# First pair's tiles in the order of work, sign rows in one VectorE instruction, the mixture's scale chain first in line

## The chip, the cores and the metric

The kernel runs on one core of a Trainium2 chip. A core has TensorE (PE, matmuls and transposes into PSUM), VectorE (DVE), ScalarE (ACT), GpSimd (POOL) and SyncE (SP, which here issues every DMA). Each engine works through its own list in order and waits on semaphores for the others. The metric is the device time of one execution in microseconds, the median of several runs. All times below are of the device.

## The reference, cut to what matters

Two layers. The first is attention for 4 batches of 8 heads over 768 positions of width 64, in which a query sees only the keys that fall into the same bucket. The bucket is the pattern of signs of six random projections:

```python
q_bits = (np.einsum('bhsd,dk->bhsk', q, proj) > 0)
k_bits = (np.einsum('bhsd,dk->bhsk', k, proj) > 0)
mask = q_bucket[:, :, :, None] == k_bucket[:, :, None, :]
scores = np.where(mask, scale * np.matmul(q, k.transpose(0, 1, 3, 2)), -1000000000.0)
attn_out = softmax(scores) @ v
```

The second is a mixture of four causal attention experts over the first layer's output `x` (4 x 768 x 512), of which each position takes the two with the largest gate:

```python
logits = x @ w_gate                      # the two largest of four, softmax over them
for e in range(E):
    q, k, v = x @ wq[e], x @ wk[e], x @ wv[e]
    ye = softmax(causal(scale * q @ k.T)) @ v @ wo[e]
    out += gate[e] * ye
```

## The kernel before, in words

The work is cut into units. `("L", b, h)` is one head of the first layer, `("M", b, e)` one expert of the second; there are 32 of the one and 16 of the other, in one sequence in which the experts of a batch stand between the heads of the next. A unit computes scores twice. `max_steps` makes them in `mx` tiles (PSUM, two buffers) and VectorE reduces each to a maximum per query (`pm`, or `pmw` for the first four heads). `shift_steps` turns the maxima into a `row` that a DMA writes under the query tile as one more contraction row. `s_unit` then makes the scores again, transposed, in `st` tiles (three buffers); ScalarE takes the exponential twice, once to fp32 (`p`) and once to fp16 (`ph`), GpSimd subtracts one from the other (`pl`, function `lo`), and TensorE multiplies `ph` and `pl` with the halves of V into `o`. `normalise` divides (`rden`, then `xp` or `yn`).

The bucket mask is part of the matmul. The six projections of q and k are made by TensorE with the small matrix `pbd`, four groups of 32 PSUM rows in one tile; `signs` turns them into 0/1 style rows and DMAs (`qk<-M`, `qk<-Mw`, `xt<-Mw`) write those under q and k, so that a score in another bucket falls out. Before the change VectorE compared and subtracted (`m0` in the code, `m` in the profile) and ScalarE scaled the result into `M`. In the very first pair of heads the four groups were worked as four instructions of 32 rows on each engine.

Heads are prepared in pairs: `prep_wide` for the first two pairs of batch 0 (fp32 tiles, named `xt` for pair 0 and `qk` for pair 1), `prep_pair` for the rest. They transpose q and k (`natq`, `natk`), split each into two parts, project and make the sign rows. `natq`, `natk`, `natv` are loaded by SP; a load waits for a mark that `FIRST` names (for instance "m", the last sign instruction). `pair_scales` finds scales from the maxima of q, k and v (`mqk`). `mixture_scales(b)` makes three numbers per batch (`xs`) that the experts need: a reciprocal and a product on VectorE in a `misc` tile of PSUM, a copy on ScalarE (`xw`), a product on VectorE (`xs<-misc,xw`), two more on ScalarE. Every transpose, projection and scale shares the two `misc` buffers.

Everything is first recorded and then put in order by `Recorder.schedule`, a list scheduler with its own costs: at each step the instruction that can start first on its engine goes, and among equals the one with the smaller number `prio`, which is the place of recording plus an entry of `PRIO` for the group that it belongs to. So every change in costs or priorities redraws the order of all engines. Until the first `o` tile the scheduler fills idle TensorE time with small matmuls `o<-ident`, as many as its own estimate of the gap asks for; they compute nothing that is used. All instructions are issued by one line of the code (L423), so the profile's rows are told apart by tiles.

Of the kernel before, what the change touches and what calls it, by code (L numbers as in the profile page):

```python
# [141 lines left out]
PRIO = {"norm": -300, "pair_scales": -100, "shift_steps": -100, "halves": 50, "weights": 400}  # L142
# [286 lines left out]
WIDE = 2.0 ** 60  # L429
LN_SHIFT = 5.545177444479562  # L430
# [7 lines left out]
FIRST = {("q", 1): None, ("k", 1): "m", ("v", 1): "row", ("q", 2): "m", ("k", 2): "m"}  # L438
# [13 lines left out]
def tile_kernel(ctx, tc, q, k, v, proj, w_gate, wq, wk, wv, wo, out):  # L452
# [75 lines left out]

    pat = con.tile([1, 3, 128], BF, name="pat")
# [3 lines left out]
    nc.gpsimd.memset(pat[:, 1], MISS)  # L533
    nc.gpsimd.memset(pat[:, 2], 1.0)
    for g in range(4):
        o = 32 * g
        if g < 2:
            nc.gpsimd.memset(pat[:, 0, o + 2 * NB:o + 2 * MR], 1.0)
        else:
            nc.gpsimd.memset(pat[:, 0, o:o + 2 * NB], 1.0)  # L540
            nc.gpsimd.memset(pat[:, 0, o + 2 * MR:o + 2 * MR + 4], -1.0)
            nc.gpsimd.memset(pat[:, 1, o + 2 * MR:o + 2 * MR + 4], UNIT)
            nc.gpsimd.memset(pat[:, 2, o:o + 2 * MR], WIDE)
# [3 lines left out]
    sub_mul = con.tile([128, 3], FT, name="sub_mul")  # L547
    nc.vector.tensor_copy(sub_mul, pp[:, 0:3])
# [6 lines left out]
    pbh = con.tile([128, 32], HF, name="pbh")  # L555
    pbl = con.tile([128, 32], HF, name="pbl")
# [155 lines left out]
    def signs(p, gs, ds, parts, M, mul, rows):  # L712

        m0 = sb.tile([128, HS], HF, name="m0", bufs=1)
        for r in parts:
            nc.vector.tensor_scalar(m0[r], p[r, :HS], 0.0, sub_mul[r, 0:1], op0=OP.is_gt, op1=OP.subtract)
            marks["m"] = nc.scalar.activation(M[r], m0[r], AF.Copy, scale=sub_mul[r, mul:mul + 1])
        for g in gs:
            a, n = (ds[g % 2]["qa"], MR) if g < 2 else (ds[g % 2]["ka"], MR + rows)
            move(a[D:D + n].rearrange("p (j s) -> p j s", j=2), M[32 * g:32 * g + 2 * n][:, None, :])  # L720

    def prep_wide(hp):
# [14 lines left out]
        for nm, h in [("q", 0), ("q", 1), ("k", 0), ("k", 1)] if hp else [("q", 0), ("k", 0), ("q", 1), ("k", 1)]:  # L737
# [17 lines left out]
            gs = () if nm == "q" else range(4) if hp and h else () if hp else (h, 2 + h)  # L755
            if gs:
                p = misc()
                for g in gs:
                    marks["p"] = nc.tensor.matmul(p[32 * g:32 * g + 32, :HS], pbd, TT["q" if g < 2 else "k"][:, g % 2],
                                                  start=True, stop=True, tile_position=(0, 32 * g))  # L760
                signs(p, gs, ds, [slice(0, 128)] if hp else [slice(32 * g, 32 * g + 32) for g in gs], M, 2, 1)
# [5 lines left out]
    def proj_halves():  # L767
# [9 lines left out]
        t = sb.tile([128, 32], FT, name="pbs", bufs=1)  # L777
# [6 lines left out]
    def prep_pair(b, hp):  # L784
# [32 lines left out]
        for n, (w, x) in enumerate(((pbh, 0), (pbl, 0), (pbh, 1))):  # L817
            for g in range(4):
                nc.tensor.matmul(p[32 * g:32 * g + 32, :HS], w, parts[g][x], start=not n, stop=n == 2,
                                 tile_position=(0, 32 * g))  # L820
        signs(p, range(4), ds, [slice(0, 128)], sb.tile([128, HS], HF, name="M", bufs=1), 1, 2)
# [158 lines left out]
    def s_unit(u):  # L980
# [477 lines left out]
```

## Time and profile before

| what | us |
|---|---|
| median of 3 runs | 663.68 (663.67 to 669.59) |
| the profiled execution | 664.07 |
| its span, first to last instruction | 662.3 |
| TensorE busy | 634.6 (96%) |
| VectorE busy | 513.4 (78%) |
| ScalarE busy | 509.1 (77%) |
| GpSimd busy | 467.2 (71%) |

Some 1.8 us of the profiled execution lie outside its span. Busy TensorE time includes the filling matmuls of the start.

### The profile page before, as it was taken

How to read it: one execution, taken by the hardware profiler on the slowest of the kernel's cores; microseconds unless marked ns; L12 is line 12 of the kernel's file. 1: busy time of each engine (PE TensorE's matmuls, PEld its weight loads, DVE VectorE, ACT ScalarE, POOL GpSimd, SP SyncE). 2: the span in 40 equal slices, each digit the busy share in tenths (PEclk: the TensorE clock that was granted, in tenths of full speed). 3: DMA queues.
4: the chain of work that ended last, by engine and by line, in shares of the span. 5: the costliest groups of instructions: out<-in, count | busy, mean ns of one | idle time of the engine just before them, and what ended most of it. 6: DMA issues, size and time to landing. Idle time of an engine off the chain costs nothing. (4 is left out here: it accounts for less than half of the span.)

```text
span 662.3 us, 21568 instructions
## 1 busy us (share of the span) xinstructions
PE 634.6 (96%) x8320; PEld 466.9 (70%) x8320; DVE 513.4 (78%) x1280; ACT 509.1 (77%) x1093; POOL 467.2 (71%) x496
## 2 busy tenths in 40 slices
PE   8999999899999999999999999999999899999996
PEld 7878777576777666677767777777767666767663
DVE  5978999899779797878978898877967569447641
ACT  3278899899968978786977889795978777942773
POOL 3088999798966967784966869784866776960662
PEclk9999999799999999999999999999999999999999
DMA  4674454434330323333052332305154012001212
GB/s 101 137 160 93 100 120 100 98 68 117 67 86 11 82 66 72 77 64 90 21 139 90 65 87 63 91 9 113 39 125 116 9 42 57 3 22 35 75 66 96
DMA packets 109923, 50.87 MB, mean 77 GB/s; under 512 B 88428, under 2 KB 105980, under 8 KB 109820
## 3 DMA queue, kind: packets, MB, share of 16 engines
q1 hardware_dynamic: 109820, 49.50, 31.9%
q8 instruction: 65, 1.06, 0.7%
q14 instruction: 38, 0.31, 0.2%
HBM read 20.98 MB, written 6.29 MB: 41 GB/s over the span
## 5 line engine op out<-in xcount | busy, mean ns | idle before, releaser
L423 POOL TENSOR_TENSOR pl<-p,ph 128x512 f16<-128x512 f32 (+2 forms) x384 | 424.1, 1128 | 168.4 <-ACT ph L423 90.2
L423 ACT ACTIVATE p<-st 128x512 f32<-128x512 f32 (+2 forms) x384 | 229.8, 599 | 45.0 <-PE st L423 38.1
L423 DVE TENSOR_REDUCE pm<-mx 128x2 f32<-128x512 f32 (+2 forms) x380 | 227.1, 616 | 23.8 <-PE mx L423 21.6
L423 PE MATMUL st<-qk 78*128 78x512 f16 (+2 forms) x976 | 227.3, 325 | 3.5 <-DMA qk<-row 2.1
L423 ACT ACTIVATE ph<-st 128x512 f16<-128x512 f32 (+2 forms) x384 | 230.3, 602 | 0.2 <-PE st L423 0.2
L423 PEld LDWEIGHTS <-ph 128*128 128x128 f16 x2976 | 157.8, 98 | 30.8 <-issue 3.4
L423 PEld LDWEIGHTS <-qk 78*128 78x128 f16 (+4 forms) x1392 | 124.5, 98 | 60.9 <-issue 12.4
L423 PE MATMUL mx<-qk 76*128 76x512 f16 (+2 forms) x488 | 136.6, 326 | 7.7 <-DVE pm L423 3.1
L423 PEld LDWEIGHTS <-pl 128*128 128x128 f16 x1488 | 136.2, 97 | 10.2 <-POOL pl L423 4.0
L423 PE MATMUL o<-vh,pl 128*128 128x65 f16 x1152 | 127.0, 194 | 2.0 <-POOL pl L423 1.4
L423 PE MATMUL o<-vh,ph 128*128 128x65 f16 x1152 | 127.7, 194 | 0.1
L423 PE MATMUL o<-vl,ph 128*128 128x64 f16 x1152 | 126.8, 192 | 0.1
L423 PE MATMUL misc<-xt,wqk_h 128*128 128x384 f16 x256 | 53.7, 326 | 0.0
L423 PEld LDWEIGHTS <-ident 128*128 128x128 bf16 x499 | 38.4, 101 | 12.0 <-issue 2.2
L423 PE MATMUL o<-mvh,ph 128*128 128x65 f16 x336 | 37.2, 194 | 0.9 <-DVE yn L423 0.6
L423 PE MATMUL o<-mvh,pl 128*128 128x65 f16 x336 | 37.5, 193 | 0.0
L423 PE MATMUL o<-mvl,ph 128*128 128x64 f16 x336 | 37.2, 192 | 0.0
L423 ACT ACTIVATE qk<-misc 128x384 f16<-128x384 f32 (+1 forms) x31 | 15.2, 489 | 28.4 <-PE misc L423 26.3
L423 PEld LDWEIGHTS <-xt 128*128 128x128 f16 x324 | 30.2, 97 | 8.6 <-ACT xt L423 0.5
L423 DVE SCALAR_TENSOR_TENSOR qk<-misc,qk 128x384 f16<-128x384 f32 (+1 forms) x34 | 18.8, 553 | 21.3 <-ACT qk L423 21.1
L423 PEld LDWEIGHTS <-wqk_h 128*128 128x128 f16 x256 | 24.3, 97 | 14.7 <-issue 0.6
L423 DVE SCALAR_TENSOR_TENSOR qk<-misc,cs,qk 128x384 f16<-128x384 f32 x56 | 32.9, 603 | 0.9 <-ACT qk L423 0.7
(181 smaller groups left out, 948.1 us busy)
## 6 DMA issues: line engine op xcount, KB each, us to landing
qk<-qk SPq DMA_DIRECT2D x128, 96.0 KB
natv<-in_v_dram SPq DMA_DIRECT2D x16, 384.0 KB
natq<-in_q_dram SPq DMA_DIRECT2D x15, 384.0 KB
natk<-in_k_dram SPq DMA_DIRECT2D x15, 384.0 KB
qk<-qk SPq DMA_DIRECT2D x112, 48.0 KB
out_dram<-ot SPq DMA_DIRECT2D x20, 256.0 KB
xt<-xt SPq DMA_DIRECT2D x8, 96.0 KB
xt<-xt SPq DMA_DIRECT2D x4, 192.0 KB
```

Of the source, the lines that this page charges most:

```text
L423: getattr(getattr(self.nc, e), m)(*[real(x) for x in args], **{k: real(x) for k, x in kw.items()})
```

## The change

Six edits. (1) `mixture_scales` gets a priority of -3000, ahead of all else that is ready. (2) `signs` becomes one VectorE instruction that compares with a small number and multiplies by a number per partition, and writes `M` itself; the ScalarE step goes. `pat`, from which the per-partition numbers are made, is filled by more small memsets, and `pbd` has a second half with negated signs. (3) The groups stand as q and k of one head, then q and k of the other, so the first pair needs one instruction of 64 rows for each head, and the DMAs go in the order q, k of the first head, q, k of the second. (4) The tiles of the first pair are taken from their ring in the order head by head. (5) The load of pair 1's k waits for mark "t" (a split) and no longer for "m". (6) In the last unit the subtraction that makes `pl` may go to VectorE or GpSimd.

```diff
-PRIO = {"norm": -300, "pair_scales": -100, "shift_steps": -100, "halves": 50, "weights": 400}
+PRIO = {"norm": -300, "pair_scales": -100, "shift_steps": -100, "halves": 50, "mixture_scales": -3000, "weights": 400}
...
+LEAST = 2.0 ** -126
...
-FIRST = {("q", 1): None, ("k", 1): "m", ("v", 1): "row", ("q", 2): "m", ("k", 2): "m"}
+FIRST = {("q", 1): None, ("k", 1): "t", ("v", 1): "row", ("q", 2): "m", ("k", 2): "m"}
...
-    pbd = con.tile([128, 32], FT, name="pbd")
+    pbd = con.tile([128, 2, 32], FT, name="pbd")
     nc.gpsimd.memset(pbd, 0.0)
     for j in range(2):
-        for r in range(2):
-            nc.vector.tensor_copy(pbd[D * j:D * j + D, 2 * NB * r + j:2 * NB * r + 2 * NB:2], pst[D * j:D * j + D])
+        for i in range(2):
+            for r in range(2):
+                x = pbd[D * j:D * j + D, i, 2 * NB * r + j:2 * NB * r + 2 * NB:2]
+                if i == r:
+                    nc.vector.tensor_copy(x, pst[D * j:D * j + D])
+                else:
+                    nc.vector.tensor_scalar(x, pst[D * j:D * j + D], -1.0, None, op0=OP.mult)
...
-    def signs(p, gs, ds, parts, M, mul, rows):
+    def signs(p, gs, ds, part, M, mul, rows):
-        m0 = sb.tile([128, HS], HF, name="m0", bufs=1)
-        for r in parts:
-            nc.vector.tensor_scalar(m0[r], p[r, :HS], 0.0, sub_mul[r, 0:1], op0=OP.is_gt, op1=OP.subtract)
-            marks["m"] = nc.scalar.activation(M[r], m0[r], AF.Copy, scale=sub_mul[r, mul:mul + 1])
+        marks["m"] = nc.vector.tensor_scalar(M[part], p[part, :HS], least_times[part, 0:1], least_times[part, mul:mul + 1],
+                                             op0=OP.is_gt, op1=OP.mult)
         for g in gs:
-            a, n = (ds[g % 2]["qa"], MR) if g < 2 else (ds[g % 2]["ka"], MR + rows)
+            a, n = (ds[g // 2]["ka"], MR + rows) if g % 2 else (ds[g // 2]["qa"], MR)
...
-        for n in "qk":
-            for d in ds:
+        for n, d in [(n, d) for n in "qk" for d in ds] if hp else [(n, d) for d in ds for n in "qk"]:
...
-                signs(p, gs, ds, [slice(0, 128)] if hp else [slice(32 * g, 32 * g + 32) for g in gs], M, 2, 1)
+                signs(p, gs, ds, slice(32 * gs[0], 32 * gs[-1] + 32), M, 2, 1)
...
-                nc.gpsimd.tensor_tensor(pl[:, :o], p32[:, :o], ph[:, :o], op=OP.subtract)
+                (nc.vector_or_gpsimd if u == seq[-1] else nc.gpsimd).tensor_tensor(pl[:, :o], p32[:, :o], ph[:, :o], op=OP.subtract)
```

How the order moves is shown at three places. Over the whole program TensorE loses 40 of its 307 filling matmuls and keeps all its other matmuls; ScalarE loses 19 sign activations; GpSimd gets 14 more memsets and gives five of the last unit's six `pl` to VectorE.

The first place is VectorE's list at the start, before the change, from the second head's signs (`m`) through the first head's nine reductions (`pmw_151`) to its row (`roww`):

```order
L423 TENSOR_SCALAR m_347<-misc,sub_mul 32x384 x2
L423 TENSOR_SCALAR qk<-misc 128x384
L423 SCALAR_TENSOR_TENSOR qk<-misc,qk 128x384
L423 TENSOR_SCALAR qk<-misc 128x384
L423 SCALAR_TENSOR_TENSOR qk<-misc,qk 128x384
L423 TENSOR_REDUCE pmw_151<-mx 128x2 x9
L423 TENSOR_REDUCE pmw_153<-mx 128x2
L423 TENSOR_REDUCE negm_138<-pmw_151 128x12
L423 TENSOR_REDUCE pmw_153<-mx 128x2 x2
L423 TENSOR_SCALAR roww<-misc 6x128
```

The same stretch of the changed kernel (its numbers for the tiles differ; `pmw_178` are the first head's maxima, `pmw_180` the second's):

```order
L423 TENSOR_SCALAR Mw<-misc,least_times 64x384
L423 TENSOR_SCALAR qk<-misc 128x384 x2
L423 SCALAR_TENSOR_TENSOR qk<-misc,qk 128x384 x2
L423 TENSOR_REDUCE pmw_178<-mx 128x2 x9
L423 TENSOR_REDUCE pmw_180<-mx 128x2
L423 TENSOR_REDUCE negm_157<-pmw_178 128x12
L423 COPY Tk<-misc 128x384
L423 TENSOR_REDUCE pmw_180<-mx 128x2
L423 TENSOR_TENSOR qk<-misc,qk 128x384 x2
L423 TENSOR_REDUCE pmw_180<-mx 128x2
L423 TENSOR_SCALAR roww<-misc 6x128
```

Two instructions of signs became one, and a copy and two splits of pair 1's k moved between the first head's maxima and its row.

The second place is SP's list of DMAs around the loads of pair 2, before the change, where `natq`, `natk` and `natv` in the second half are pair 2's and `qk<-Mw` are pair 1's sign rows:

```order
L423 DMA natv<-in_v_dram 128x12x64
L423 DMA xt<-xt 64x384 x2
L423 DMA qk<-Mw 12x2x384 x2
L423 DMA qk<-Mw 13x2x384 x2
L423 DMA natq<-in_q_dram 128x12x64
L423 DMA xt<-roww 1x6x128
L423 DMA fq_113<-fr 2x6x128
L423 DMA xt<-xt 64x768
L423 DMA natk<-in_k_dram 128x12x64
```

And in the changed kernel:

```order
L423 DMA natv<-in_v_dram 128x12x64
L423 DMA qk<-Mw 12x2x384
L423 DMA qk<-Mw 13x2x384
L423 DMA qk<-Mw 12x2x384
L423 DMA qk<-Mw 13x2x384
L423 DMA xt<-xt 64x384 x2
L423 DMA natq<-in_q_dram 128x12x64
L423 DMA natk<-in_k_dram 128x12x64
```

The sign rows alternate q and k, and the load of pair 2's k stands right behind that of q, ahead of three DMAs that it followed.

The third place is VectorE's list in batch 1, before the change, from the second instruction of `mixture_scales` (`misc<-misc,rw`) to the one that frees its `misc` tile (`xs<-misc,xw`):

```order
L423 TENSOR_SCALAR misc<-misc,rw 128x1
L423 SCALAR_TENSOR_TENSOR xt<-misc,xs,xt 128x3x128
L423 TENSOR_SCALAR up<-misc,lower 12x128
L423 SCALAR_TENSOR_TENSOR row<-misc,up 12x128
L423 TENSOR_REDUCE mqk<-natq 128x1
L423 TENSOR_SCALAR rden<-o,cs_2259 128x6
L423 RECIPROCAL rden<-rden 128x6
L423 TENSOR_TENSOR xp<-o,rden 128x6x64
L423 TENSOR_REDUCE mqk<-natk 128x1
L423 TENSOR_REDUCE pm_147<-mx 128x2 x2
L423 TENSOR_TENSOR xs<-misc,xw 128x1
```

And in the changed kernel, from the chain's first instruction:

```order
L423 RECIPROCAL misc<-xs 128x1
L423 TENSOR_TENSOR rden<-o,gw 128x6
L423 SCALAR_TENSOR_TENSOR qk<-misc,cs_2277,qk 128x384
L423 TENSOR_SCALAR misc<-misc,rw 128x1
L423 TENSOR_TENSOR yn<-o,rden 128x6x64
L423 TENSOR_TENSOR xs<-misc,xw 128x1
```

Ten instructions stood between the two before, one does now. In batch 3 it is 19 before and two after.

## Rows read from the trace of the kernel before

**Rows 1.** The page, part 1: busy time by engine, share of the span, instructions.

```profile
PE 634.6 (96%) x8320; PEld 466.9 (70%) x8320; DVE 513.4 (78%) x1280; ACT 509.1 (77%) x1093; POOL 467.2 (71%) x496
```

**Rows 2.** Engines by stretch: length, busy us (instructions), then clock, DMA share, GB/s.

```profile
40.00:60.00 20.00, 18.74 (x229) 15.54 (x228) 16.39 (x37) 15.18 (x32) 15.95 (x16) 0.91 0.56 118
80.00:100.00 20.00, 19.78 (x286) 14.53 (x285) 19.94 (x39) 19.04 (x40) 18.21 (x17) 1.00 0.54 117
120.00:140.00 20.00, 18.17 (x196) 12.43 (x194) 17.27 (x39) 17.35 (x38) 17.04 (x16) 0.83 0.30 66
140.00:160.00 20.00, 18.39 (x231) 12.52 (x230) 17.05 (x37) 18.35 (x47) 16.72 (x18) 1.00 0.56 126
```

**Rows 3.** Whom TensorE waited for: us in total, times, longest us.

```profile
PE st L423 <- DMA qk<-row: 2.1, 2, 1.2
...
PE o L423 <- POOL pl L423: 1.4, 3, 0.6
```

**Rows 4.** Timeline of the start: start us, length us, what [idle before <-releaser].

```profile
7.65 0.49 PE L423 MATMUL misc<-ident,natk 128*128 128x128 f32 x3
12.15 1.23 ACT L423 ACTIVATE Mw<-m,sub_mul 32x384 fp32r<-32x384 f16 x2
12.77 1.99 SPq L423 DMA_DIRECT2D xt<-Mw  x2
16.72 0.71 PE L423 MATMUL mx<-xt 76*128 76x512 f32 x3
18.37 6.30 DVE L423 TENSOR_REDUCE pmw<-mx 128x2 f32<-128x512 f32 x9
26.68 0.27 DVE L423 TENSOR_SCALAR roww<-misc 6x128 fp32r<-6x128 f32 x1
34.19 0.15 DVE L423 TENSOR_SCALAR cs<-misc 128x1 int32<-128x1 int32 x1
```

**Rows 5.** Timeline around pair 2's k: its load, its maximum, TensorE's next `mx`.

```profile
38.78 0.53 SPq L423 DMA_DIRECT2D natk<-in_k_dram  x1
44.22 0.95 DVE L423 TENSOR_REDUCE mqk<-natk 128x1 bf16<-128x768 f32 x1 [1.28 <-DMA natk<-in_k_dram]
45.82 0.50 PE L423 MATMUL mx<-qk 76*128 76x256 f32 x2 [1.18 <-DVE pmw L423]
```

**Rows 6.** Instructions that touch tile `M`: ns min/median/max, first and last start us.

```profile
L423 SPq DMA_DIRECT2D qk<-M x56: 782/822/1554, 64.1 to 540.0; - x56
L423 ACT ACTIVATE M<-m,sub_mul x14: 598/615/645, 63.5 to 536.7; 128x384 f16<-128x384 f16 x14
```

**Rows 7.** Timeline: one pair's sign rows, and two `mx` behind such rows.

```profile
118.64 0.38 PE L423 MATMUL mx<-qk 76*128 76x512 f16 x1 [0.81 <-PE o L423]
...
142.11 0.61 DVE L423 TENSOR_SCALAR m<-misc,sub_mul 128x384 f16<-128x384 f32 x1
143.38 0.60 ACT L423 ACTIVATE M<-m,sub_mul 128x384 f16<-128x384 f16 x1
...
149.75 0.59 PE L423 MATMUL mx<-qk 76*128 76x512 f16 x3 [1.49 <-DMA qk<-M]
```

**Rows 8.** Timeline, batch 3: `mixture_scales` from its first instruction, and TensorE after it.

```profile
511.41 0.15 DVE L423 RECIPROCAL misc<-xs 128x1 f32<-128x1 f32 x1
523.21 0.16 DVE L423 TENSOR_TENSOR xs<-misc,xw 128x1 f32<-128x1 f32 x1 [1.88 <-ACT xw L423]
528.12 0.55 PE L423 MATMUL misc<-ident,xp 128*128 128x128 f32 x3 [1.00 <-DVE qk L423]
```

**Rows 9.** Timeline of the end: last unit's exponentials and `pl`, the division, what follows.

```profile
643.58 6.01 POOL L423 TENSOR_TENSOR pl<-p,ph 128x512 f16<-128x512 f32 x6 [0.53 <-ACT ph L423]
647.21 0.50 ACT L423 ACTIVATE ph<-st 128x256 f16<-128x256 f32 x1
650.11 0.17 DVE L423 TENSOR_SCALAR rden<-o 128x6 f32<-128x6 f32 x1 [3.96 <-PE o L423]
651.35 0.33 PE L423 MATMUL misc<-ident,yn 128*128 128x128 f32 x1 [0.64 <-DVE yn L423]
```

More of the change, by code (lines that the diff above doesn't have):

```diff
@@ L532, in tile_kernel @@
     nc.gpsimd.memset(pat[:, 0], 0.0)
-    nc.gpsimd.memset(pat[:, 1], MISS)
-    nc.gpsimd.memset(pat[:, 2], 1.0)
     for g in range(4):
         o = 32 * g
-        if g < 2:
-            nc.gpsimd.memset(pat[:, 0, o + 2 * NB:o + 2 * MR], 1.0)
+        if g % 2 == 0:
+            nc.gpsimd.memset(pat[:, 0, o + 2 * NB:o + 2 * MR], -LEAST)
+            for i in (1, 2):
+                nc.gpsimd.memset(pat[:, i, o:o + 2 * NB], MISS if i == 1 else 1.0)
+                nc.gpsimd.memset(pat[:, i, o + 2 * NB:o + 32], -MISS if i == 1 else -1.0)
         else:
-            nc.gpsimd.memset(pat[:, 0, o:o + 2 * NB], 1.0)
+            nc.gpsimd.memset(pat[:, 0, o:o + 2 * NB], -LEAST)
             nc.gpsimd.memset(pat[:, 0, o + 2 * MR:o + 2 * MR + 4], -1.0)
-            nc.gpsimd.memset(pat[:, 1, o + 2 * MR:o + 2 * MR + 4], UNIT)
-            nc.gpsimd.memset(pat[:, 2, o:o + 2 * MR], WIDE)
+            for i, (x, y) in ((1, (MISS, UNIT)), (2, (WIDE, 1.0))):
+                nc.gpsimd.memset(pat[:, i, o:o + 2 * NB], -x)
+                nc.gpsimd.memset(pat[:, i, o + 2 * NB:o + 2 * MR], x)
+                nc.gpsimd.memset(pat[:, i, o + 2 * MR:o + 32], y)
     pp = misc()
@@ L546, in tile_kernel @@
         nc.tensor.matmul(pp[:, i:i + 1], pat[:, i], one16[:, 0:1], start=True, stop=True)
[L547 to L549 removed]
+    least_times = con.tile([128, 3], FT, name="least_times")
+    nc.vector.tensor_copy(least_times, pp[:, 0:3])
+    pbd = con.tile([128, 2, 32], FT, name="pbd")
     nc.gpsimd.memset(pbd, 0.0)
     for j in range(2):
[L552 to L556 removed]
+        for i in range(2):
[5 more added lines that the diff above has]
+                    nc.vector.tensor_scalar(x, pst[D * j:D * j + D], -1.0, None, op0=OP.mult)
+    pbh = con.tile([128, 2, 32], HF, name="pbh")
+    pbl = con.tile([128, 2, 32], HF, name="pbl")
     NV = 2
@@ L754, in prep_wide @@
             nc.sync.dma_start(raw(a[lo, od]), raw(a[hi, ev]))
-            gs = () if nm == "q" else range(4) if hp and h else () if hp else (h, 2 + h)
+            gs = () if nm == "q" else range(4) if hp and h else () if hp else (2 * h, 2 * h + 1)
             if gs:
@@ L758, in prep_wide @@
                 for g in gs:
-                    marks["p"] = nc.tensor.matmul(p[32 * g:32 * g + 32, :HS], pbd, TT["q" if g < 2 else "k"][:, g % 2],
+                    marks["p"] = nc.tensor.matmul(p[32 * g:32 * g + 32, :HS], pbd[:, g % 2], TT["qk"[g % 2]][:, g // 2],
                                                   start=True, stop=True, tile_position=(0, 32 * g))
-                signs(p, gs, ds, [slice(0, 128)] if hp else [slice(32 * g, 32 * g + 32) for g in gs], M, 2, 1)
+                signs(p, gs, ds, slice(32 * gs[0], 32 * gs[-1] + 32), M, 2, 1)
             yield 109 * (NT // 2)
@@ L776, in proj_halves @@
         scale_of([mx], c[:, 0:1])
-        t = sb.tile([128, 32], FT, name="pbs", bufs=1)
+        t = sb.tile([128, 2, 32], FT, name="pbs", bufs=1)
         nc.scalar.activation(t, pbd, AF.Copy, scale=c[:, 0:1])
@@ L818, in prep_pair @@
             for g in range(4):
-                nc.tensor.matmul(p[32 * g:32 * g + 32, :HS], w, parts[g][x], start=not n, stop=n == 2,
+                nc.tensor.matmul(p[32 * g:32 * g + 32, :HS], w[:, g % 2], parts[2 * (g % 2) + g // 2][x], start=not n, stop=n == 2,
                                  tile_position=(0, 32 * g))
-        signs(p, range(4), ds, [slice(0, 128)], sb.tile([128, HS], HF, name="M", bufs=1), 1, 2)
+        signs(p, range(4), ds, slice(0, 128), sb.tile([128, HS], HF, name="M", bufs=1), 1, 2)
         marks["m", b, hp] = marks["m"]
```

## The prediction

> **What bounds the kernel now.** I read the page's busy times first, then the stretches, then the list of what TensorE waited for, and last the timeline at the longest waits. TensorE is busy 634.6 of 662.3 us [rows 1], so it is the bound and it is idle for 27.7 us; about 5 of them are the last DMAs. The busy time also holds the 307 filling matmuls of the start. The change takes none of TensorE's other matmuls away, so it can win only four things: a shorter start, waits of TensorE in the middle, stretches at the lower clock, and a shorter end. Removing ScalarE work for its own sake (19 sign instructions, 14 of them at 0.615 us [rows 6]) pays nothing, because ScalarE's mean load is 77%. The reader should note two more things. VectorE is as full as TensorE between 80 and 100 us, 19.94 against 19.78 of 20 [rows 2], so there is no room there for more VectorE work. And the granted clock was 0.91 of full speed over 40 to 60 us and 0.83 over 120 to 140 us [rows 2]. If the lower of the two levels is half (1.2 of 2.4 GHz), the first is 0.09 x 20 x 2 = 3.6 us at half speed and the second 0.17 x 20 x 2 = 6.8 us, which cost a full TensorE 1.8 and 3.4 us.
>
> **A, the start: -1.2 us.** The first head's k is transposed at 7.65 us, its sign rows pass VectorE and then ScalarE until 13.38 (12.15 + 1.23), are sent from 12.77 on, and the first `mx` matmul runs at 16.72; VectorE starts the nine reductions at 18.37, over a microsecond after their input, since it first splits pair 1's q [rows 4]. In the new order TensorE does the first k after 6 fillers instead of 34 and a wait for the second head's q. But the sign rows stand behind four `xt<-xt` copies on SP, one of which needs the second head's k, so they leave only about 0.5 us earlier. VectorE is what gains: two sign instructions of 0.62 us fewer [rows 7], against four more small `pbd` instructions of 0.2 us; two casts go to ScalarE. I put the reductions at 17.3, 1.1 us earlier. On the way to the first row the order gives most of this back: a copy and two splits (some 0.55 us each) now stand in front of `roww`, so it comes at 26.7 to 27.5, against 26.68 [rows 4]. What lets the first `o` matmul go is the scale of v, `cs` at 34.19 [rows 4]; before it stand nine reductions of the second head in the old order and eight in the new, so this path keeps the 1.1 us and wins part of one reduction (6.30 / 9 = 0.7 us) [rows 4], less the 0.5 of the copy. Hence -1.2. Bounds: -2.5 if nothing is given back, and +0.8 if the row decides. The 14 more memsets lie beside waits for the first loads; uncovered they cost under 1 us, for they stand ahead of the numbers per partition that the first sign instruction needs.
>
> **B, pair 2's k: -1.2 us.** Its load was issued at 38.78; VectorE stood 1.28 us waiting for it at 44.22, and TensorE then 1.18 us for VectorE [rows 5]. In the new order this load follows pair 2's q directly, ahead of three DMAs. Pair 1's sign rows no longer pass ScalarE, and I estimate an issue some 4 us earlier, while VectorE asks for it only about 1 to 3 us earlier. The wait goes; next late is v of the same pair, which did not stop VectorE before. Bounds: -1.2 to 0.
>
> **C, sign rows in the other pairs: -1.5 us.** VectorE ended the comparison at 142.72, ScalarE its scaling at 143.98 [rows 7]: 1.3 us there, and 0.62 at least, since ScalarE's own instruction takes 0.615 [rows 6]. The new instruction has the same shape as the old on VectorE, so I cost it at the same 0.61. One sign DMA holds SP for 0.82 us [rows 6] and k of the pair's first head goes second instead of third. The first head's `mx` can start about 1.5 to 2 us earlier, the second head's q rows come at about the old time. Two waits of TensorE hang on this: 1.49 us at 149.75, ended by `qk<-M`, and 0.81 us at 118.64 [rows 7], which the profile puts down to TensorE itself and which I take for a DMA as well. I count the first whole and nothing of the second. Bounds: -2.3 to 0.
>
> **D, the mixture's scales: -1.5 us.** In batch 3 the chain's first instruction ran at 511.41 and the one that frees its `misc` tile at 523.21 [rows 8]: one of two buffers held for 11.8 us, because the ScalarE step was put behind exponentials, and VectorE stood 1.88 us for it. After it TensorE waited 1.00 us at 528.12 [rows 8] and three times for `pl`, 1.4 us in all [rows 3]. In the new order two instructions of VectorE stand between the same two, not 19. I take the wait of 1.0 and a third of the others. Bounds: -2.4 to 0; the waits for `pl` may be GpSimd's own.
>
> **E, the end: -0.6 us.** GpSimd works off the last six `pl` from 643.58 to 649.59, though the last exponential ends at 647.71; the last division starts at 650.11, and TensorE stands 0.64 us for it at 651.35 [rows 9]. With five of six on VectorE, which is idle there for 3.96 us [rows 9], the last `o` matmuls go ahead of four output matmuls, and these cover the division. I count the 0.64 and no more, since TensorE is full otherwise. Bounds: -0.9 to 0. No row shows VectorE and GpSimd side by side in this step. The Trainium skill (SBUF — State Buffer, section "SBUF: two separate sides") says that a VectorE instruction with two SBUF inputs and a GpSimd instruction that reads SBUF exclude each other for their whole length. By that the one `pl` left on GpSimd could hold VectorE for its whole length, E would be 0 and the sum 659.0; no run here shows it yet.
>
> **F, the clock: -1.8 us.** A half-speed stretch followed the wait at 45.82 and another the waits around 118 to 123, but none followed the longest wait, at 149.75: the clock was 1.00 over 140 to 160 [rows 2, 5, 7]. So a wait does not suffice to bring one, and I count only the first, whose wait goes by B: -1.8. Bounds: -5.2 to 0.
>
> **G, new waits: +2.1 us.** The order after the start is drawn anew on every engine. Stretches like 80 to 100 us, idle 0.22 of 20 [rows 2], can only lose. I charge one wait of the size seen (1.2 us) and half the price of a half-speed stretch of the shorter kind (0.9). Bounds: 0 to +5, two waits and the longer stretch.
>
> **Sum.** 664.07 (the profiled execution) - 1.2 - 1.2 - 1.5 - 1.5 - 0.6 - 1.8 + 2.1 = 658.4. That execution lay 0.4 above the median of 663.68, so I predict 658.0, 0.9% faster. A change of 1%, 6.6 us, is about what a measurement of this kernel can tell from none.
>
> **Rivals.** *All of it pays.* Both half-speed stretches go and no long wait is new: A to E in full measure with C at -2.3 and D at -2.4, F at -5.2: 664.1 - 1.2 - 1.2 - 2.3 - 2.4 - 0.6 - 5.2 = 651.2, 650.8 by the median; with part of G some 653. For it: the waits of 118 to 123 us stand in the stretch where one of them is C's. Against: the 1.2 us wait there is for a `row` [rows 3], which C moves only through the maxima.
>
> *The waits move.* The sequence of units is unchanged and TensorE is full; a wait that goes here comes back at the next late DMA or `pl`. Then A and E stay: 664.1 - 1.2 - 0.6 - 0.4 = 661.9. For it: TensorE's waits are many and small; `row` with 2.1 us in two waits and `pl` with 1.4 in three [rows 3] are a small part of the 22 that are left without the last DMAs. Against: B and D are single places with a named cause that the order removes.
>
> *Slower: the start runs dry.* The planner took 40 fillers out because by its own costs the work comes sooner. If the first row comes late (A at +0.8), TensorE idles between 27 and 37 us where fillers ran, and the clock falls to half for two stretches as long as the one in 120 to 140 us (3.4 us each) in the dense part behind it. With B, C, D and E paying 4.8 and nothing of F: 664.1 + 0.8 + 6.8 - 4.8 - 0.4 = 666.5. It decides from the point where the first row is over 0.8 us later than 26.68. Against: 32 of the remaining fillers stand just before the first `st`.
>
> **How the numbers follow.** Forecast 0.34, all of it pays 0.31, the waits move 0.27, slower 0.08. Of the forecast's own spread (656 to 660.5) about a third lies below 657.0, the bound of 1%. Faster by over 1%: 0.31 + 0.11 = 0.42. Slower by over 1% (670.3) needs the last rival and a third long stretch: 0.03. Within 1%: 0.55. The range goes from the second case with half of its clock gain lost, 651.5, to the third with a new short stretch at half speed (1.8 us), 664; the slower rival and the very best draw stay out.
>
> **What would show it.** A: first reductions near 17.3 and the first `o` matmul near 36. B: no wait of VectorE for `natk` near 42, and clock 1.00 over 40 to 60. C: no `mx` that waits for `qk<-M`. D: under 4 us between `misc<-xs` and `xs<-misc,xw` in each batch. E: the last division under 2 us after the last exponential, and no wait of TensorE behind it. What would make it wrong: a clock below 0.95 in another stretch, TensorE idle before the first `o`, or a new long `pl` or DMA wait in 150 to 500 us.

## The result and the profile after

Over 19 executions of each kernel the median went from 669.96 us (663.03 to 675.43) to 659.28 us (654.54 to 665.49); the ratio is 0.9857, 95% interval 0.9823 to 0.9892. So the change made the kernel 1.4% faster, where 0.9% was forecast. The absolute forecast of 658.0 fits more closely than that, because the median of three that it started from, 663.68, lies at the low end of the 19 executions of before. The profiled executions took 664.07 and 656.76 us, so of the 10.7 us between the medians the two profiles hold 7.3; the readings below explain those.

First the page's busy times and the stretches of the changed kernel (columns as in [rows 1, 2]). TensorE lost 8.8 us of busy time, 40 fillers among them.

```profile
PE 625.8 (96%) x8280; PEld 462.6 (71%) x8280; DVE 510.2 (78%) x1274; ACT 500.3 (76%) x1087; POOL 462.5 (71%) x505
```

```profile
40.00:60.00 20.00, 18.44 (x247) 14.71 (x247) 17.00 (x44) 16.22 (x35) 16.71 (x17) 1.00 0.63 134
80.00:100.00 20.00, 18.03 (x254) 12.79 (x253) 17.70 (x35) 17.23 (x37) 16.85 (x17) 1.00 0.54 123
120.00:140.00 20.00, 19.01 (x252) 12.84 (x251) 18.78 (x45) 18.86 (x42) 17.99 (x17) 1.00 0.57 123
140.00:160.00 20.00, 19.52 (x265) 13.81 (x261) 18.73 (x40) 18.84 (x48) 16.49 (x19) 1.00 0.43 105
420.00:430.00 10.00, 7.61 (x102) 5.75 (x99) 7.09 (x20) 6.42 (x15) 5.84 (x7) 0.83 0.20 48
```

Read the clock column: both stretches that were below 1.00 before are at 1.00, and 420 to 430 is the new one. In the kernel before the half-speed stretches were 47.5 to 50.9 and 122.6 to 129.4 us, in the changed kernel 425.8 to 429.2; each of the three has a row of its own here, at 0.50 or 0.51 of full speed, the lower of the two levels. Before:

```profile
47.50:50.90 3.40, 3.40 (x24) 3.21 (x22) 2.73 (x8) 1.63 (x4) 1.16 (x1) 0.50 0.74 159
122.60:129.40 6.80, 6.36 (x38) 4.00 (x38) 5.36 (x12) 4.29 (x10) 4.87 (x5) 0.50 0.45 100
```

and after:

```profile
425.80:429.20 3.40, 3.40 (x44) 2.88 (x43) 2.84 (x9) 2.55 (x6) 1.60 (x2) 0.51 0.02 5
```

TensorE's waits after [rows 3 is the same view]: the list has a new head, the waits behind the maxima `mqk`, which came to 2.3 us in three waits before, and the wait for `qk<-M` has doubled from 1.5 us.

```profile
PE misc L423 <- DVE mqk L423: 4.8, 4, 1.9
PE mx L423 <- DMA qk<-M: 3.1, 2, 1.6
...
PE st L423 <- DMA qk<-row: 1.3, 1, 1.3
```

The start after, timeline [rows 4, 5]. The first k, the sign rows, the reductions and the first `o` matmul are all earlier, the last by 3.3 us (37.09 before); k of pair 2 is issued 4.5 us earlier, and VectorE finds it landed.

```profile
5.43 0.73 PE L423 MATMUL misc<-ident,natk 128*128 128x128 f32 x3
8.74 0.67 DVE L423 TENSOR_SCALAR Mw<-misc,least_times 64x384 fp32r<-64x384 f32 x1 [0.57 <-PE misc L423]
16.29 7.11 DVE L423 TENSOR_REDUCE pmw<-mx 128x2 f32<-128x512 f32 x10 [0.20 <-PE mx L423]
26.01 0.27 DVE L423 TENSOR_SCALAR roww<-misc 6x128 fp32r<-6x128 f32 x1
33.79 0.20 PE L423 MATMUL o<-vh,ph 128*128 128x65 f16 x1
34.31 0.69 SPq L423 DMA_DIRECT2D natk<-in_k_dram  x1
39.99 0.93 DVE L423 TENSOR_REDUCE mqk<-natk 128x1 bf16<-128x768 f32 x1
47.42 0.20 PE L423 MATMUL o<-vh,ph 128*128 128x65 f16 x1 [1.21 <-DVE pmw L423]
```

Later places of the timeline: two `mx` that wait for sign rows [rows 7], TensorE behind the maximum of `natv`, the chain of batch 3 [rows 8], and the end [rows 9].

```profile
91.06 0.59 PE L423 MATMUL mx<-qk 76*128 76x512 f16 x3 [1.50 <-DMA qk<-M]
423.86 0.23 PE L423 MATMUL misc<-ident,mqk 128*128 128x128 bf16 x1 [1.89 <-DVE mqk L423]
509.30 0.16 DVE L423 RECIPROCAL misc<-xs 128x1 f32<-128x1 f32 x1
510.72 0.15 DVE L423 TENSOR_TENSOR xs<-misc,xw 128x1 f32<-128x1 f32 x1
529.33 0.49 PE L423 MATMUL mx<-qk 76*128 76x512 f16 x2 [1.63 <-DMA qk<-M]
640.70 1.16 POOL L423 TENSOR_TENSOR pl<-p,ph 128x512 f16<-128x512 f32 x1 [3.47 <-ACT ph L423]
641.38 0.51 ACT L423 ACTIVATE ph<-st 128x256 f16<-128x256 f32 x1
643.42 0.17 DVE L423 TENSOR_SCALAR rden<-o 128x6 f32<-128x6 f32 x1 [0.81 <-PE o L423]
644.73 0.27 PE L423 MATMUL misc<-ident,yn 128*128 128x128 f32 x1
```

To see where time is won and lost I lined the kernels up by work: TensorE's matmuls without the fillers, summed by columns from the trace, an fp32 column counted as two. The lead of a kernel at a time t of the kernel before is t minus the time at which the other has begun the same share of that work. Counting an fp32 column as one or as four moves the column at 400 by up to 0.9 us, that at 520 by up to 1.3, and none from 560 on. In us:

```
edits in the kernel          60   115   160   360   400   520   560   640   655
after (all)                 3.8   2.7   6.4   6.2   5.1   2.3   4.7   5.8   6.7
b_prio (1)                 -0.1  -0.3   2.1   0.7  -2.1  -1.3   2.9   3.7   3.7
b_end (6)                  -0.6  -1.1  -2.8  -3.2  -3.5  -6.9  -6.9  -6.7  -5.8
b_first (4,5)               2.0   2.2   6.2   6.1   3.2   0.6   0.6   1.3   1.3
signs (2,3)                 2.8   2.1   5.6  -1.7 -18.4 -20.4 -16.2 -15.3 -15.3
signs_prio (1,2,3)          2.7   2.1   5.9   3.2  -1.5  -4.1   0.3   1.2   1.2
a_noprio (2-6)              3.2   3.1   7.6   5.8   1.3  -2.5   1.7   2.8   3.6
a_nosigns (1,4-6)           2.7   3.2   7.9   0.9   0.1  -1.0   3.3   4.2   5.1
a_hop (all, two steps)      3.5   4.1   8.2   0.0  -0.7  -2.5   1.8   2.7   3.6
b_w74 (none, new draw)      1.4   1.8   6.6  -3.7 -20.9 -25.9 -21.3 -20.5 -20.5
a_vt (all, v early)         3.5   2.5   0.6   3.1   3.4   4.6   8.0   8.9   9.8
a_vt_w74 (same, new draw)   4.0   3.4   1.6   3.0   3.3   4.8   7.9   8.8   9.7
a_vt_b2 (v early late on)   2.2   1.2   5.9   9.7  10.0  11.1  15.0  15.9  16.8
```

The first line is the result in parts: 3.8 us from the start, 1.1 of them lost by 115, 3.7 more by 160 (the second half-speed stretch of before, 6.8 us long, costs 3.4), 4.1 lost between 160 and 520 and 2.4 won between 520 and 560 (each within the 1.3 us of the counting; 1.7 lost in the two together), 1.1 won before the end and 0.9 in it. The rest of the table is the experiments.

### The profile page after: what moved, and what is told of

It is laid out like the page before. It is cut to its first block, busy times and chain, and to the rows that moved or that the text cites. A ratio compares the mean times of both kernels' runs of the same rounds, so it can differ in the third digit from the quotient of the medians.

```text
span 654.9 us, 21470 instructions
## 1 busy us (share of the span) xinstructions
PE 625.8 (96%) x8280; PEld 462.6 (71%) x8280; DVE 510.2 (78%) x1274; ACT 500.3 (76%) x1087; POOL 462.5 (71%) x505
## 4 chain that ended last, share of the span: by engine, by line
PE 69%; DVE 14%; DMA 8%; ACT 3%; issue 2%; SPq 2%; POOL 2%; POOLq 0%; ACTq 0%; DVEq 0%
PE misc L423 24%; PE st L423 18%; PE o L423 17%; PE mx L423 10%; DVE pm L423 6%; DMA natv<-in_v_dram 5%; DVE qk L423 2%; SPq L423 2%; ACT p L423 1%; DVE mqk L423 1%; DMA qk<-M 1%; POOL pl L423 1%; ACT ph L423 1%; DVE misc L423 1%; DMA xt<-xt 1%
## 5 line engine op out<-in xcount | busy, mean ns | idle before, releaser
L423 POOL TENSOR_TENSOR pl<-p,ph 128x512 f16<-128x512 f32 x379 | 419.3, 1130 | 165.5 <-ACT ph L423 74.8
L423 PEld LDWEIGHTS <-qk 78*128 78x128 f16 (+4 forms) x1392 | 123.7, 98 | 57.5 <-issue 10.2
L423 PE MATMUL o<-vh,ph 128*128 128x65 f16 x1152 | 125.5, 194 | 2.5 <-DVE xp L423 1.3
L423 PEld LDWEIGHTS <-ident 128*128 128x128 bf16 x459 | 35.5, 100 | 11.9 <-issue 2.7
L423 PEld LDWEIGHTS <-xt 128*128 128x128 f16 x324 | 30.5, 97 | 10.1 <-issue 1.2
```

Of the source, the lines that this page charges most:

```text
L423: getattr(getattr(self.nc, e), m)(*[real(x) for x in args], **{k: real(x) for k, x in kw.items()})
```

## The experiments

Theory: the gain is that of named places, the start with pair 2's k, the mixture's chain, the end. Rival: every edit makes the planner draw up a new order (a draw, below), and what the draw brings outweighs the places. Each ratio is against executions of the kernel before on the same chip and at the same time; their median was 669.47, 665.67 and 666.99 us in the three sessions, so ratios of different sessions compare less well than their intervals say.

**Parts of the change, alone.** Edit (1) into the kernel before, `b_prio`:

```diff
+PRIO = {..., "mixture_scales": -3000, ...}
```

> The kernel before with edit (1) alone, the priority of the mixture's scales; the order of TensorE is the old one for about the first 200 us, so the half-speed stretch near 47 us and the waits of the start stay. Theory 1, every named term pays by itself: under 4 us between misc<-xs and xs<-misc,xw in all four batches (11.8 in batch 3 before), no wait of 1 us near 528, and 1.5 to 2.5 us of lead over the kernel before that appear between 500 and 560 us; ratio 0.996 to 0.998. Rival, the gain belongs to the order as it falls out: the holds are short here too, but the lead is spent again at other waits, and the ratio lies anywhere from 0.99 to 1.01 whatever the chain does.

Ratio 0.9964 (0.9926 to 1.0002). The holds (the time from `misc<-xs` to `xs<-misc,xw`, for which the chain keeps one of the two `misc` buffers) were 1.1, 1.4, 1.0 and 1.4 us (1.1, 6.9, 2.7 and 11.8 before). TensorE over 515 to 535 us, first the kernel before, then `b_prio`:

```profile
515.00:525.00 10.00, 9.18 (x175) 7.18 (x171) 4.68 (x15) 8.86 (x21) 10.00 (x10) 1.00 0.03 7
525.00:535.00 10.00, 8.19 (x105) 6.03 (x105) 7.54 (x17) 7.67 (x18) 4.84 (x6) 1.00 0.05 13
```

```profile
515.00:525.00 10.00, 10.00 (x151) 7.95 (x150) 9.97 (x25) 10.00 (x23) 9.91 (x10) 1.00 0.07 15
525.00:535.00 10.00, 10.00 (x124) 6.76 (x125) 5.25 (x13) 7.61 (x16) 7.16 (x8) 1.00 0.08 19
```

With the hold of 11.8 us, TensorE idled 0.82 + 1.81 = 2.6 us in these 20 us, and all of it is gone here. The table points the same way: from 520 to 560 the two kernels that keep this hold (`b_end`, `b_first`) win 0.0, all others 2.4 to 4.6. But those two also run the order of the kernel before there (`b_first` from 231 us on, on every engine), and `b_prio` has a new order from 213 us on. So it isn't shown that the hold alone cost the 2.6 us. The rival holds for the sum: `b_prio` lost 2.8 us between 360 and 400, of which a new half-speed stretch of 3.4 us at 395 explains 1.7.

Edit (6) into the kernel before, `b_end`:

```diff
-nc.gpsimd.tensor_tensor(pl[:, :o], ...)
+(nc.vector_or_gpsimd if u == seq[-1] else nc.gpsimd).tensor_tensor(pl[:, :o], ...)
```

> The kernel before with edit (6) alone; every engine's order is the old one up to the last unit. Theory 1: the last division comes about 1.5 us after the last exponential (2.4 before), TensorE has no wait behind it, and the stretch from the last exponential to the end of the span is 0.6 to 0.9 us shorter; ratio 0.9985 to 0.9995. Rival, the two engines hold each other up over the operands: VectorE's pl instructions take as long as the GpSimd one beside them (over 1.1 us each instead of 0.7) and the end gains under 0.2 us; ratio 1.000.

Ratio 0.9916 (0.9875 to 0.9958). This run shows two things. The place does what was said: between 640 and 655 all eight kernels with edit (6) win 0.8 or 0.9 us and the five without it 0.0. And the comparison is coarser than its interval: up to the last unit this kernel runs the order of before, instruction by instruction, its place is worth 0.14% (0.9 of 664 us), and it came out 0.84% faster, though its profiled execution was 6.9 us behind at 520, half of that by half-speed stretches of 3.4 us at 151 and 434 that the profiled execution of before doesn't have.

Edits (4) and (5), `b_first`:

```diff
-FIRST = {..., ("k", 1): "m", ...}
+FIRST = {..., ("k", 1): "t", ...}
...
-        for n in "qk":
-            for d in ds:
+        for n, d in [(n, d) for n in "qk" for d in ds] if hp else [(n, d) for d in ds for n in "qk"]:
```

> The kernel before with edits (4) and (5) alone: the ring of the first pair's tiles head by head and the load of pair 1's k behind mark t. The sign rows still go through VectorE and ScalarE as four instructions each. Theory 1: the load of pair 1's k and with it pair 2's is issued 1 to 3 us earlier, the start gains 0 to 1 us by the first o matmul (37.09 before); ratio 0.998 to 1.000, and most of the start's gain is missing because the sign rows were its cause. Rival, the order as it falls out: the time moves by more than 0.3% either way with the half-speed stretches and the waits of the middle, although the first o matmul moves by less than 1 us.

Ratio 0.9844 (0.9791 to 0.9896), as fast as the whole change (its profiled execution, 662.55 us, is the slowest of its six). It has the old sign rows, the old chain (holds of 8.8 and 11.8 us) and a first `o` matmul that is later than before, at 38.67 us. VectorE finds pair 2's k landed at 35.2 (before it waited 1.28 at 44.22), and neither of the two early half-speed stretches is there. The rival's condition held: a gain of 1.6% that the start up to the first `o` doesn't show. Its order from 231 us on is that of the kernel before, so what its order wins is won ahead of that: the lead is 6.2 us at 160.

Edits (2) and (3), `signs`:

```diff
-        nc.vector.tensor_scalar(m0[r], p[r, :HS], 0.0, sub_mul[r, 0:1], op0=OP.is_gt, op1=OP.subtract)
-        marks["m"] = nc.scalar.activation(M[r], m0[r], AF.Copy, scale=sub_mul[r, mul:mul + 1])
+        marks["m"] = nc.vector.tensor_scalar(M[part], p[part, :HS], least_times[part, 0:1],
+                                             least_times[part, mul:mul + 1], op0=OP.is_gt, op1=OP.mult)
```

> The kernel before with edits (2) and (3) alone: sign rows by one VectorE instruction and each head's q and k side by side; the old priorities, ring order, load mark and end. Theory 1: first reductions near 16.5 to 17.3, first o matmul 2 to 3 us before 37.09, no wait for natk in pair 2; the holds of the mixture's chain are as long as before in one batch (over 6 us) and the last division 2.4 us after the last exponential; ratio 0.991 to 0.994, that is the whole gain less some 3 us of chain and end. Rival, the order as it falls out: the start gains the same 2 to 3 us, but the time differs from that sum by over 3 us, with clock stretches or waits that none of the edits names.

Ratio 1.0212 (1.0158 to 1.0266), 2.1% slower. The start came much as expected (first reductions 17.16, lead 2.8 at 60 us; the first `o` at 35.9, 1.2 us earlier than before where 2 to 3 were expected), and then the lead fell by 16.7 us between 360 and 400. Timeline of the chain of batch 2 in this kernel, and the stretches behind it:

```profile
364.03 0.16 DVE L423 RECIPROCAL misc<-xs 128x1 f32<-128x1 f32 x1
382.75 0.47 ACT L423 ACTIVATE xw<-misc 128x1 f32<-128x1 f32 x1
383.24 0.16 DVE L423 TENSOR_TENSOR xs<-misc,xw 128x1 f32<-128x1 f32 x1 [5.14 <-ACT xw L423]
```

```profile
380.00:400.00 20.00, 14.90 (x159) 9.56 (x157) 8.55 (x18) 9.05 (x21) 7.02 (x8) 0.91 0.15 34
400.00:420.00 20.00, 16.54 (x135) 9.45 (x133) 17.74 (x38) 10.40 (x23) 9.62 (x10) 0.74 0.42 88
```

The small ScalarE step `xw` stood behind 35 exponentials. One of the two `misc` buffers was held for 19.2 us, then VectorE stood 5.14 us at the product, with the splits that prepare the next units behind it on its queue. TensorE was idle for 5.1 + 3.5 us, and half-speed stretches of 3.4 and 10.2 us (at 392.7 and 409.8) took 6.8 more: 15.4 of the 16.7.

**Is it the chain?** Edits (1) to (3), `signs_prio`, differ from `signs` by the priority alone:

```diff
+PRIO = {..., "mixture_scales": -3000, ...}
```

> Edits (2), (3) and (1) together: the kernel that was 2.1% slower, with the mixture's scales first in line. Theory 1: no wait of VectorE for xw, holds under 4 us in every batch, the 18 us of lead lost between 240 and 400 us shrink to under 6, ratio 0.985 to 1.000. Rival, the sign rows themselves cost the time (they add a DMA-heavy stretch and a fuller VectorE): the chain is short but the ratio stays over 1.010.

Ratio 0.9856 (0.9797 to 0.9915), 3.5% below `signs`. Holds 1.2, 1.5, 1.0 and 1.2 us, no wait for `xw`; it lost 4.7 us between 360 and 400, not 16.7. So the sign rows by themselves don't bring the loss; with the chain first in line, in the order that follows from it, most of it is gone.

The opposite, the changed kernel without edit (1), `a_noprio`:

```diff
-PRIO = {..., "mixture_scales": -3000, ...}
```

> The changed kernel without edit (1): the mixture's scales have their old priority again; the order is the changed kernel's for the first 200 us. Theory 1, the chain is a hazard that any new order can trip over (as in the run of edits 2 and 3 alone, where VectorE stood 5.1 us for xw behind a row of exponentials and TensorE lost over 10 us between 370 and 400): some batch holds misc<-xs to xs<-misc,xw for over 5 us and this run is 2 to 12 us slower than the changed kernel, ratio 0.990 to 1.004. Rival, the chain matters for 2 us at most and the rest is the order as it falls out: ratio 0.984 to 0.990, whatever the holds.

Ratio 0.985 (0.9807 to 0.9893): the rival's number. One hold was 6.2 us (batch 1), but none stood in a place where it cost anything visible. So the priority is an insurance. All six kernels with the old priority have a hold of over 6 us: in two it was 19.2 us, with 15 us lost around it, in three 11.8 us, with 2.6 us of idle TensorE behind it, in this one it cost nothing visible. With the priority no hold in eight kernels was longer than 2.9 us.

**Is it the sign rows?** The changed kernel without edits (2) and (3), `a_nosigns`, so in `signs`

```diff
-        marks["m"] = nc.vector.tensor_scalar(M[part], p[part, :HS], least_times[part, 0:1], ...)
+        nc.vector.tensor_scalar(m0[r], p[r, :HS], 0.0, sub_mul[r, 0:1], op0=OP.is_gt, op1=OP.subtract)
+        marks["m"] = nc.scalar.activation(M[r], m0[r], AF.Copy, scale=sub_mul[r, mul:mul + 1])
```

> The changed kernel without edits (2) and (3): sign rows over VectorE and ScalarE again, four instructions for the first pair, old order of groups; edits (1), (4), (5), (6) stay. Theory 1, the sign rows carry the start and the waits for qk<-M: first o matmul 2 to 4 us later than the 33.79 of the changed kernel, and 3 to 5 us slower in all, ratio 0.990 to 0.994. Rival, the load mark and the ring order (0.984 alone) carry the gain through the half-speed stretches at 47 and 122 us that go away with them: ratio 0.976 to 0.986, as fast as the changed kernel or faster although its first o matmul is later.

Ratio 0.9881 (0.9832 to 0.9929), between the two expectations and against 0.9857 (0.9823 to 0.9892) with them: not to be told apart. The first `o` matmul was at 38.7 us, 4.9 later than in the changed kernel, and the lead at 115 us was 3.2, against 2.7. And with only the second step put back, `a_hop`:

```diff
+        m0 = sb.tile([128, HS], HF, name="m0", bufs=1)
+        nc.vector.tensor_scalar(m0[part], p[part, :HS], least_times[part, 0:1], None, op0=OP.is_gt)
+        marks["m"] = nc.scalar.activation(M[part], m0[part], AF.Copy, scale=least_times[part, mul:mul + 1])
```

> The changed kernel with the sign rows made in two steps again, a comparison on VectorE and the multiplication on ScalarE, and all else of the change kept (one instruction of 64 rows for each head of the first pair, q and k side by side, ring, load mark, priority, end). Theory 1, the second engine is what the sign rows cost: first reductions near 17, first o matmul 0.5 to 1.5 us after 33.79, and 1 to 3 us slower than the changed kernel in all; ratio 0.988 to 0.991. Rival, by the first eight runs the lead at 100 us is 2 to 3 us with either kind of sign row, so the step saved is spent before the next DMA lands: first o matmul later, lead at 100 us the same, ratio 0.983 to 0.988.

Ratio 0.9888 (0.9855 to 0.9921), inside the first expectation and 0.0008 from the rival's, with an interval that covers both; nor can it be told from the changed kernel's. First reductions at 16.24, first `o` at 37.45 (3.7 us later, where 0.5 to 1.5 were expected), and a lead of 4.1 at 115 us, as the rival has it: by then the step saved has been spent. TensorE waited 0.4 us in all for `qk<-M` here and 3.1 in the changed kernel, but not once in `a_noprio`, which has the same sign rows as the changed kernel. The second engine isn't what these waits come from.

**How large is a draw?** `b_w74`:

```diff
-WAIT = 75.0
+WAIT = 74.0
```

> The kernel before with the planner's allowance for a wait at 74 ns, not 75: nothing is taken away or added, only the order of all engines behind the start is drawn anew. This is the size of the draw itself. Theory 1, the named causes make the gain: holds of the mixture's chain stay (over 5 us in some batch), waits for natk near 44 stay, ratio 0.996 to 1.004. Rival, any new draw of the order moves the time by as much as the whole change: ratio outside 0.992 to 1.008 on either side.

Ratio 1.0295 (1.0261 to 1.0328), although nothing but a constant of the planner moved. The rival, then, but with a named place: the chain of batch 2 was held for the same 19.2 us as in `signs`, and VectorE stood the same 5.14 us for it. (The planner came to the same order there, 37 VectorE and 404 TensorE instructions in a row from the chain's first on, so the two runs show one such place and not two.)

```profile
366.10 0.16 DVE L423 RECIPROCAL misc<-xs 128x1 f32<-128x1 f32 x1
385.31 0.16 DVE L423 TENSOR_TENSOR xs<-misc,xw 128x1 f32<-128x1 f32 x1 [5.14 <-ACT xw L423]
```

The lead fell by 17.2 us between 360 and 400. The start tells against the named places in the other direction: with none of the edits this kernel leads by 6.6 us at 160, as much as the changed kernel (6.4). Pair 2's k is loaded almost when it was before (38.78), yet VectorE doesn't wait for it, and neither early half-speed stretch is there (two lines of the timeline and a stretch):

```profile
38.39 0.39 SPq L423 DMA_DIRECT2D natk<-in_k_dram  x1
43.29 0.95 DVE L423 TENSOR_REDUCE mqk<-natk 128x1 bf16<-128x768 f32 x1
40.00:60.00 20.00, 19.68 (x284) 16.12 (x283) 18.46 (x43) 18.59 (x38) 19.08 (x18) 1.00 0.64 131
```

So of the changed kernel's 6.4 us at 160, no part is shown to need these edits rather than a new order.

**The new wait, for v.** In the changed kernel the load of v stands on SyncE behind four sign DMAs and eleven copies: at 418.69 us, where k of the same pair went at 403.92. `a_vt` lets it go at a split, in batches 1 to 3 (batch 0 stays as it was):

```diff
-        g = FIRST.get((nm, hp), "m" if nm == "v" else "t") if not b else "m" if nm == "v" else "t"
+        g = FIRST.get((nm, hp), "m" if nm == "v" else "t") if not b else "t"
```

> The changed kernel, and the load of v in all pairs but the first waits for the mark of a split (t) instead of the last sign instruction (m), so that on SyncE it stands ahead of the four sign DMAs and about ten copies that it stands behind now. Theory 1, the waits for natv (8.7 us of VectorE, 4.8 us of TensorE behind mqk, and the half-speed stretch at 425.8) cost the changed kernel 3 to 6 us: the waits of TensorE behind mqk fall under 2 us, ratio 0.977 to 0.982. Rival, each transfer that goes earlier makes the sign rows or the row later on the same queue: TensorE's waits for qk<-M and qk<-row grow by as much, ratio 0.984 to 0.990.

Ratio 0.9789 (0.9742 to 0.9836). TensorE's waits behind `mqk` fell from 4.8 us to none that the list shows. Part of it was paid at other places as the rival said: 2.0 us for one `qk<-row` in batch 1, at 133 us, and a half-speed stretch of 6.8 behind it; the lead fell from 5.8 at 130 us to 0.6 at 160. Behind 160 it rose by 9.2, where the changed kernel's rose by 0.3. The same kernel with another draw, `a_vt_w74` (WAIT at 74):

> The kernel with v of batches 1 to 3 loaded behind a split (0.979), with the planner's allowance at 74 ns, so that its order is drawn anew from about 200 us on. If its gain came from the cause named (no wait of TensorE behind mqk), it is in this draw too: waits behind mqk under 1 us and a ratio of 0.974 to 0.984. Rival, it was the draw: 0.985 or more.

Ratio 0.9804 (0.9775 to 0.9834), and a lead within 0.3 us of `a_vt`'s in the columns from 360 on. That isn't the test it was meant to be: the orders of the two differ mostly between 220 and 300 us and are the same behind, on every engine, but for two matmuls of TensorE that change places. Between 160 and 360, where they differ, the lead rose by 2.5 and 1.4 us; in the changed kernel it fell by 0.2. Last, v early in batches 2 and 3 alone, `a_vt_b2`:

```diff
+        g = FIRST.get((nm, hp), "m" if nm == "v" else "t") if not b else "m" if nm == "v" and b < 2 else "t"
```

> The changed kernel, with v loaded behind a split in batches 2 and 3 alone, so that the order of the changed kernel stays up to batch 2's loads. With v early in batches 1 to 3 the lead over the kernel before fell from 5.8 us at 130 to -1.1 at 220 and then rose by 10.9 to the end, while the changed kernel kept 4.3 at 220 and gained 2.4 behind it. Theory 1, the loss there is the price of the early load (a wait for a row at 133, a half-speed stretch behind it) and the gain behind it is the mechanism: both good parts together give 646 to 651 us, ratio 0.970 to 0.976. Rival, the draw behind 200 us spends it: ratio 0.977 to 0.984, no better than before.

Median 646.85 us, ratio 0.9715 (0.9685 to 0.9744), faster than both kernels. Its profile has no half-speed stretch before the end, and TensorE's waits, in the view of [rows 3], are short. Behind them a stretch of the changed kernel, then the same of this one:

```profile
PE mx L423 <- DMA qk<-M: 1.5, 2, 1.2
PE mx L423 <- DVE pm L423: 1.2, 4, 0.4
```

```profile
160.00:520.00 360.00, 350.12 (x4688) 258.63 (x4684) 294.73 (x755) 286.61 (x626) 266.01 (x254) 1.00 0.31 73
160.00:520.00 360.00, 357.80 (x4825) 263.96 (x4822) 299.24 (x765) 296.49 (x641) 275.44 (x264) 1.00 0.33 73
```

TensorE idles 2.2 us there instead of 9.9. Of the 7.7 between them 4.4 are waits behind `mqk`, and the half-speed stretch at 425.8 was worth 1.7 more; the remaining 3 or so are other waits that this order doesn't have, and that they hang on v isn't shown. From 301 us of `a_vt` on its order is that of `a_vt` too, so the gain there (6.7 us from 360 on in both runs of `a_vt`'s kind, 7.1 here, 0.5 in the changed kernel) is that of one order, seen three times.

## Why the prediction was right, and where it was not

**A, the start.** The events came earlier than I put them (reductions 16.29 for 17.3, first `o` 33.79 for 36), yet A, B and the first half-speed stretch together gave 3.8 us by 60, against 1.2 + 1.2 + 1.8 = 4.2. The step of A that failed was to price it by the first `o` matmul. Between `a_hop`, `a_nosigns` and the changed kernel it moves by 4.9 us and the lead at 115 doesn't follow; the later two are ahead there.

**B and the first part of F.** The waits and the stretch went as forecast, and they are tied together more closely than I had put it: pair 2's wait for k stands at 44 to 45 us in the kernel before, `b_prio` and `b_end` (1.28, 1.28 and 1.9 us), each of the three has a half-speed stretch at 47 to 49, and none of the other eleven profiles has the wait or a stretch there. That the one brings the other isn't shown: the changed kernel has a wait of 1.21 us at 47.42 and stays at 1.00. Nor is it shown that the earlier load is what it takes, since `b_w74` gets rid of both with the load 0.4 us earlier. The second stretch is another matter: `b_prio`, with the order of before up to some 210 us, doesn't have it. F was -1.8 in the forecast; the profile shows -5.1 for both and +1.7 for the new one.

**C, the sign rows.** Wrong, for its sign too. I took the ScalarE hop for the cause of the waits for `qk<-M`. The two waits of [rows 7] went, and two of 1.50 and 1.63 us stand elsewhere. With the hop kept, `a_hop` has 0.4 us of them, and with the new rows `a_noprio` has none, so they come and go with the order and not with the step. What the step saved is also a small part of the path: at the wait of 91.06 the rows were ready at 86.09 (85.43 + 0.66), and the other 5 us went to the sign DMAs, of which the second ended the wait:

```profile
85.43 0.66 DVE L423 TENSOR_SCALAR M<-misc,least_times 128x384 f16<-128x384 f32 x1
86.30 3.53 SPq L423 DMA_DIRECT2D qk<-M  x4
```

The new instruction also isn't as cheap as the old one: 655 to 678 ns, where I had 0.61 us.

**D, the chain.** Right mechanism as far as shown, size too small: with the hold of batch 3 went 2.6 us, not 1.5, and over the bound of 2.4. I misread the waits for `pl`: of the three one stands at 577.57, far behind, and one ended at 522.43, before the chain did; what I left out were the waits for ScalarE and for GpSimd's other work at 525 to 532. And I priced the edit by the one draw at hand, while its larger worth is that a later draw doesn't bring a hold of 19.2 us, as far as eight kernels show it.

**E, the end.** Right: 0.8 or 0.9 us for 0.6, in all eight kernels. The row shows the division 1.5 us after the last exponential and no wait behind it.

**G, new waits.** Of the size charged in kind, but named wrongly: I expected a wait "of the size seen" anywhere and wrote of v only that it had not stopped VectorE before. It was v: 4.8 us of TensorE in four waits, one followed by a half-speed stretch, where the kernel before had 2.3 us in three, which I had not counted; so 2.5 are new. Two of the signs that I had named for being wrong came here: a clock of 0.83 over 420 to 430 us, and a long wait (1.89 us) in front of it. Between 160 and 520 us the changed kernel lost 4.1 us, of which that stretch, counted under F, is 1.7.

**The sum.** 664.07 to 656.76 in the profiles, 658.4 forecast. F won 1.6 us more than charged, D 1.1 and E 0.3, A and B 0.3 less; what is left for C and G together is +1.7, where -1.5 + 2.1 = +0.6 stood. So two terms lie outside their bounds, D (2.6 for at most 2.4) and C (its waits grew by 1.6, where nothing was the worst). That the total came within 1.6 us is in part luck: F, D and E won 3.0 more than charged, and the others 1.4 less. By `b_end` the comparison itself can be off by 0.7%, half of the gain. The lower end of the range, 651.5, doesn't follow from its own words either: 650.8 with half of the clock's 5.2 lost is 653.4; the measured time lies above both. And the mechanism behind the number is right for the end, likely for the chain, and open for the start, where `b_w74` has the same gain without the edits.

## What to carry to other kernels

A tiny step that holds a shared buffer belongs at the head of its queue whatever it costs now: read how long each such buffer is held in every batch, and price the edit by the longest hold that another order could give, not by the one in the trace. Where a scheduler redraws the order, line the kernels up by work done and compare places, not totals; a single edit's total carries waits and half-speed stretches that it didn't ask for. After a change read the list of waits again: acting on its new head (here v's load behind sign rows on SyncE) came with as much again as the change, 6.1 of the 10.1 us at the places named. And before a gain is put down to an edit, redraw the kernel before with no edit at all: here that alone gave the start's 6.6 us, and lost 27 elsewhere.

## What the hardware showed that I had not expected

VectorE was held up beside GpSimd, by a little. In the changed kernel VectorE's `pl` of 384 columns took 835 ns beside GpSimd's last one (641.44 and 640.70 us, 0.42 us in common). Those of 512 and 256 columns, with none of GpSimd's beside them, took 693 and 412 ns, so some 0.55 us, their mean, was to be expected: 0.28 more, while GpSimd's kept its 1.16 us. All eight kernels with edit (6) have the same, 833 to 839 ns beside 0.42 us in common; none has the 384 columns alone or another overlap, so the cause is likely and not shown. A rule of the Trainium skill cited in the prediction (SBUF — State Buffer, "SBUF: two separate sides") has the two exclude each other; by that the later one waits out the 0.42 us in common. The row agrees with it if the part of the instruction that doesn't grow with the columns (0.13 us, an estimate from the 693 and 412 ns) can pass during the wait: 0.42 less 0.13 is about the 0.28 found. It did not reach E.

```profile
L423 DVE TENSOR_TENSOR pl<-p,ph x5: 412/693/835, 637.7 to 642.2; 128x512 f16<-128x512 f32 x3, 128x384 f16<-128x384 f32 x1, 128x256 f16<-128x256 f32 x1
```

The granted clock is no fixed property of an order: with one and the same order up to some 210 us, two of three profiled executions have the half-speed stretch at 122 to 130 us (the kernel before and `b_end`), the third (`b_prio`) has none. And the times of one kernel follow it in the main: among the 19 executions of the changed kernel are 654.54 us at a mean granted clock of 0.999, 659.28 at 0.994 and 664.17 at 0.986.
